# Three small jobs moved between engines, a later weight load and a new fixed order in an attention and FFT-MLP kernel

## The chip, the cores and the metric

The kernel runs on one core of one Trainium2 chip. The metric is the time of one execution in microseconds (us) on the device. Executions of one kernel mostly agree within a few tenths of a per cent to one per cent; now and then one is slower by over 1.5% (the slow state), and comparisons here use fast runs alone. TensorE multiplies matrices; VectorE, ScalarE and GpSimd (PE, DVE, ACT and POOL in the profile) do the rest; SyncE (SP) and GpSimd ask for transfers. "L926" is a line of the kernel. Where experiments have other line numbers, a longer order list has pushed the code down by six or seven lines.

## The reference, cut to what matters

```python
# attention, 4 batches, 8 heads, 768 tokens, 48 columns a head
for t in range(S):
    cur = einsum('bhd,bhe->bhde', u[None] * kt, vt)
    y[:, :, t] = einsum('bhd,bhde->bhe', rt, state + cur)
    state = wt[..., None] * state + einsum('bhd,bhe->bhde', kt, vt)
# x = y as (batch, 768, 384)
u  = x + real(fft(fft(x, axis=1), axis=2))          # mix over tokens and columns, residual
un = (u - mean(u)) / sqrt(var(u) + 1e-6)            # rows of 384
out = u + maximum(un @ w_ch1, 0) @ w_ch2            # w_ch1 is 384 x 1536, w_ch2 1536 x 384
```

## The kernel before

The recurrence is worked off in chunks of 128 tokens, six to a batch, c0 to c23. A chunk needs running sums of the logarithm of the decay w. The mix is done by matmuls with cosine and sine tables. Each row block of 128 tokens (n0 to n23) is then normed, transposed and multiplied with W1 and W2. Rows 15 to 17 and 21 to 23 are transposed by a DMA, the others by matmuls on TensorE. Four pieces concern us.

```python
# running sums of chunk n: one matmul, and a second one unless the chunk is in TCD
op("pe", "cum", ... matmul(ps(tce), MSK, L) ...)
if not tcd:
    op("pe", "cum", ... matmul(ps(tci), NLE, L) ...)           # L619
if tcd:
    op("dve", "tcd", ... tensor_tensor(out=e2, in0=ps(tce), in1=L, op=add) ...)   # L636
    op("act", "exp4", ...); op("act", "exp", ...); op("act", "expn", ...)
else:
    op("act", "exp2", ...)
# [...]
# row n: mix, residual, statistics, normed row, transpose, evacuation
op("pe", "mm", ...)                                            # 3 matmuls, L853
op("dve", "uf", ... add mix and residual ...)                  # L862
op("dve", "bns", ...); op("dve", "bna", ...)                   # L866, L868
op("act", "un", ... Identity(scale=-1, bias=agg mean) ...)     # L418
op("pe", "trn", ...); op("act", "ev384", ... unt <- bank ...)  # L889, L901
# [...]
ws, WN = [], ((6, "w"), (6, "w"))      # W1 and W2 are asked for after chunk 6's w load
```

Nothing is scheduled while the kernel runs. A list ORDER holds some 1,540 operations; every engine works off its own operations in the order of that list, and waits on semaphores where an input or a buffer isn't ready. BANKS says in which of eight PSUM banks each matmul result goes. A search made both lists.

Of the kernel before, what the change touches and what calls it, by code (L numbers as in the profile page):

```python
# [5 lines left out]
ALU = mybir.AluOpType  # L6
ACTF = mybir.ActivationFunctionType
# [5 lines left out]
    0, 3, 4, 74, 8, 9, 5, 7, 75, 17, 15, 13, 1, 39, 30, 76, 12, 18, 77, 24, 49, 11, 10, 47,  # L13
    31, 1511, 19, 59, 48, 40, 1512, 32, 1513, 20, 78, 1514, 41, 60, 22, 21, 109, 1515, 64, 25, 23, 1516, 61, 33,
    110, 34, 26, 35, 1517, 27, 28, 14, 63, 1518, 52, 29, 111, 55, 79, 36, 2, 38, 53, 6, 112, 56, 50, 51,
    37, 45, 81, 88, 141, 42, 43, 113, 46, 83, 92, 82, 142, 115, 54, 114, 84, 65, 85, 116, 117, 93, 143, 86,
    120, 80, 71, 118, 125, 87, 144, 124, 68, 89, 94, 119, 73, 126, 127, 173, 72, 96, 121, 44, 70, 102, 90, 95,
    145, 174, 103, 97, 57, 134, 129, 122, 175, 128, 98, 146, 58, 1519, 135, 123, 130, 99, 176, 69, 1520, 100, 152, 148,
    147, 131, 205, 177, 101, 1521, 66, 91, 178, 157, 179, 67, 206, 149, 1522, 133, 180, 153, 104, 150, 105, 132, 207, 151,
    156, 184, 159, 16, 158, 181, 106, 136, 208, 154, 182, 160, 166, 189, 185, 161, 137, 237, 167, 183, 209, 108, 191, 190,  # L20
    162, 211, 213, 238, 107, 210, 193, 155, 163, 138, 192, 239, 1523, 214, 139, 216, 266, 164, 215, 288, 194, 289, 290, 240,
    165, 212, 1524, 140, 195, 186, 217, 1525, 444, 241, 197, 291, 168, 188, 187, 169, 196, 445, 221, 198, 170, 267, 446, 222,
    1526, 220, 246, 1527, 171, 199, 242, 243, 447, 224, 244, 172, 218, 277, 200, 250, 251, 201, 226, 264, 245, 278, 1528, 202,
    252, 223, 247, 230, 203, 225, 292, 254, 231, 448, 253, 219, 268, 248, 256, 227, 1529, 255, 454, 228, 449, 293, 279, 451,
    229, 294, 257, 249, 458, 459, 295, 269, 232, 259, 204, 1530, 450, 455, 258, 452, 233, 453, 296, 297, 460, 280, 234, 456,
    270, 260, 281, 235, 1531, 261, 236, 461, 298, 299, 271, 463, 462, 262, 282, 272, 263, 300, 464, 273, 301, 283, 274, 302,
    265, 303, 304, 275, 284, 305, 285, 465, 286, 326, 276, 467, 317, 306, 308, 327, 457, 309, 466, 328, 318, 310, 329, 307,
    346, 468, 337, 311, 287, 319, 355, 1532, 330, 473, 1533, 312, 356, 474, 347, 331, 338, 313, 475, 332, 1534, 320, 339, 476,
    314, 321, 333, 471, 334, 357, 322, 1535, 340, 1536, 323, 315, 358, 316, 324, 469, 1537, 348, 325, 472, 1538, 1539, 378, 359,
    341, 372, 349, 366, 342, 368, 360, 470, 343, 350, 386, 369, 388, 351, 361, 382, 367, 389, 352, 362, 502, 62, 370, 379,  # L30
    376, 387, 384, 477, 377, 363, 353, 344, 374, 354, 345, 503, 380, 375, 479, 383, 419, 504, 373, 481, 483, 417, 385, 423,
    482, 505, 371, 484, 427, 381, 478, 531, 335, 395, 424, 489, 485, 336, 506, 415, 532, 480, 396, 486, 487, 488, 508, 533,
    418, 510, 428, 512, 491, 511, 490, 507, 421, 492, 534, 513, 390, 509, 493, 566, 517, 391, 535, 518, 514, 422, 497, 416,
    567, 519, 420, 515, 537, 499, 494, 568, 539, 520, 496, 541, 540, 397, 522, 495, 569, 392, 364, 542, 521, 536, 545, 500,
    601, 393, 547, 400, 570, 543, 538, 602, 498, 572, 516, 523, 544, 546, 574, 549, 398, 394, 401, 576, 551, 525, 548, 365,
    526, 603, 524, 550, 405, 577, 575, 528, 402, 604, 527, 605, 582, 578, 552, 501, 798, 607, 571, 411, 609, 579, 554, 799,
    584, 553, 413, 616, 586, 800, 403, 573, 558, 610, 406, 606, 409, 559, 801, 412, 407, 581, 608, 561, 414, 828, 615, 583,
    580, 425, 560, 585, 529, 829, 555, 564, 408, 562, 587, 410, 611, 830, 614, 617, 588, 434, 619, 530, 563, 618, 426, 399,
    429, 557, 809, 620, 612, 435, 802, 831, 556, 832, 565, 589, 648, 640, 621, 813, 613, 858, 649, 593, 623, 430, 810, 594,
    859, 641, 622, 590, 404, 596, 632, 431, 592, 591, 860, 833, 843, 834, 595, 624, 599, 439, 861, 597, 862, 625, 598, 440,  # L40
    811, 600, 888, 803, 835, 642, 633, 627, 804, 889, 650, 634, 651, 805, 643, 836, 436, 806, 890, 837, 626, 441, 807, 630,
    628, 808, 652, 653, 891, 635, 437, 629, 654, 636, 655, 637, 432, 631, 638, 644, 656, 838, 814, 815, 433, 645, 657, 680,
    646, 442, 658, 659, 662, 924, 816, 660, 844, 639, 671, 823, 818, 663, 845, 664, 824, 925, 681, 873, 682, 665, 846, 817,
    683, 647, 848, 672, 926, 700, 673, 666, 839, 819, 847, 709, 927, 684, 691, 849, 710, 701, 667, 661, 674, 820, 668, 960,
    692, 869, 685, 675, 693, 686, 669, 702, 825, 670, 443, 687, 676, 812, 822, 677, 850, 821, 688, 961, 840, 678, 711, 679,
    863, 703, 864, 826, 928, 962, 712, 899, 722, 892, 851, 734, 903, 963, 740, 865, 900, 689, 723, 438, 827, 738, 866, 868,
    852, 732, 870, 741, 1157, 867, 730, 841, 733, 720, 875, 694, 735, 1158, 726, 713, 964, 901, 935, 728, 731, 1159, 727, 704,
    742, 721, 1160, 695, 842, 724, 743, 871, 853, 877, 725, 1187, 874, 736, 969, 739, 714, 893, 854, 879, 856, 1188, 729, 883,
    936, 855, 876, 690, 894, 715, 744, 1189, 895, 878, 970, 705, 745, 884, 896, 737, 1190, 857, 880, 898, 872, 696, 749, 897,
    882, 1215, 697, 905, 750, 904, 1161, 885, 1216, 939, 929, 902, 930, 906, 937, 907, 908, 698, 971, 1217, 1168, 751, 909, 881,  # L50
    746, 706, 1218, 931, 972, 718, 910, 699, 747, 938, 754, 932, 934, 911, 748, 973, 707, 941, 716, 912, 933, 886, 1243, 708,
    913, 940, 755, 1169, 717, 752, 1244, 1191, 942, 916, 914, 944, 1198, 779, 1245, 887, 943, 1170, 780, 965, 1246, 759, 1199, 945,
    966, 765, 917, 760, 1277, 761, 967, 915, 919, 719, 949, 766, 1278, 767, 950, 968, 946, 918, 768, 763, 1279, 762, 947, 975,
    773, 1219, 951, 1280, 781, 1226, 948, 771, 782, 974, 753, 977, 1172, 923, 769, 1200, 764, 1162, 1227, 979, 1163, 1311, 976, 1164,
    952, 774, 777, 920, 1165, 978, 953, 921, 756, 770, 922, 1167, 980, 955, 757, 772, 999, 783, 778, 982, 758, 1174, 1202, 775,
    1312, 981, 1166, 1007, 1192, 776, 1000, 954, 1008, 991, 1009, 1193, 983, 1173, 957, 788, 1258, 984, 959, 992, 1194, 1182, 784, 986,
    1183, 1195, 1247, 1184, 789, 1230, 985, 1197, 1010, 1176, 956, 1175, 987, 1178, 785, 958, 989, 1177, 1001, 988, 1011, 993, 786, 994,
    1196, 995, 1012, 996, 990, 1002, 1013, 1179, 997, 1203, 1204, 1014, 1228, 1015, 1003, 1205, 1016, 1017, 1018, 1004, 1180, 790, 1005, 998,
    1181, 1019, 1039, 1288, 1021, 1206, 1030, 1281, 791, 1040, 1031, 1032, 1022, 1020, 1220, 1033, 1023, 792, 1041, 1006, 1059, 1024, 1068, 1313,
    793, 1171, 1034, 787, 1025, 1221, 794, 1035, 1042, 1036, 1207, 1026, 1043, 1027, 1069, 1037, 1060, 1209, 1070, 1038, 1061, 795, 1320, 1044,  # L60
    1062, 1045, 1028, 1071, 1050, 1051, 1029, 1289, 1222, 1046, 1052, 1048, 1210, 1047, 1208, 1248, 1249, 1223, 1185, 1225, 1095, 1053, 1224, 1232,
    796, 1079, 1096, 1101, 1231, 1254, 1234, 1097, 1250, 1186, 1087, 1253, 1054, 1081, 1080, 1260, 1233, 1088, 1063, 1083, 1251, 1102, 1055, 1211,
    1085, 1321, 1082, 1072, 1238, 1262, 1098, 1093, 1212, 1084, 1229, 1089, 1252, 1064, 1073, 1056, 1065, 1091, 1086, 797, 1259, 1255, 1099, 1239,
    1092, 1261, 1235, 1094, 1074, 1201, 1256, 1103, 1049, 1075, 1237, 1066, 1314, 1213, 1108, 1090, 1240, 1067, 1292, 1113, 1214, 1057, 1322, 1282,
    1100, 1283, 1076, 1236, 1263, 1109, 1284, 1290, 1104, 1058, 1287, 1265, 1285, 1315, 1294, 1110, 1286, 1264, 1114, 1257, 1293, 1296, 1316, 1105,
    1317, 1323, 1269, 1111, 1319, 1295, 1122, 1106, 1318, 1326, 1266, 1324, 1120, 1270, 1107, 1267, 1118, 1121, 1328, 1325, 1241, 1123, 1124, 1271,
# [221 lines left out]
def bass_rwkv6_finch__then__fnet_fourier_mix_kernel(  # L288
# [11 lines left out]
    DM = H * D  # L300
# [92 lines left out]
    def ps(t):  # L393
        return BANK[t.bank]
# [629 lines left out]
```

## Time and profile before

| | before |
|---|---|
| three runs, median (lowest to highest) | 196.43 us (195.55 to 197.74) |
| profiled span, clock of TensorE | 193.5 us, 1.000 of full |
| TensorE work and filler matmuls by the distance of their starts, idle | 157.5, 8.6, 24.7 us |
| first product with W1 | 43.9 us |
| W2 asked for, landed, first used | 36.5, 48.0, 52.7 us |

The prediction shows the lines. A group line reads: line, engine, operation, result from inputs, count, then total busy time in us and mean of one in ns, then the engine's idle time just before, and who ended it. To divide the whole span I use one more view, VectorE's start times: one residual add (L862) of each batch, the first one of batch 0 and that of row 0 of batches 1, 2 and 3. In the kernel before they come at 38.75, 83.98, 124.72 and 162.59 us, and the last matmul ends at 190.85. The recorded expectations call all of them first residual adds. That holds for batch 1; in batch 2 row 0's add is the second, and in batch 3 the third (the first ones come at 124.26 and 160.64 us). Where it matters, the text gives the first ones too.

### The profile page before, as it was taken

How to read it: one execution, taken by the hardware profiler on the slowest of the kernel's cores; microseconds unless marked ns; L12 is line 12 of the kernel's file. 1: busy time of each engine (PE TensorE's matmuls, PEld its weight loads, DVE VectorE, ACT ScalarE, POOL GpSimd, SP SyncE). 2: the span in 40 equal slices, each digit the busy share in tenths (PEclk: the TensorE clock that was granted, in tenths of full speed). 3: DMA queues.
4: the chain of work that ended last, by engine and by line, in shares of the span. 5: the costliest groups of instructions: out<-in, count | busy, mean ns of one | idle time of the engine just before them, and what ended most of it. 6: DMA issues, size and time to landing. Idle time of an engine off the chain costs nothing.

```text
span 193.5 us, 4590 instructions
## 1 busy us (share of the span) xinstructions
PE 180.0 (93%) x1730; PEld 114.7 (59%) x1730; DVE 152.1 (79%) x356; ACT 137.8 (71%) x333; POOL 118.3 (61%) x148
## 2 busy tenths in 40 slices
PE   4979899999999999998999998999979999979994
PEld 2446466755666566565767675666656566545663
DVE  8799689697258999999999999999989969800043
ACT  7899867656997794499999897488855344769400
POOL 1679789920689996899799988639375461000000
PEclk9999999999999999999999999999999999999999
DMA  5999899699989989889899991242735020140024
GB/s 118 225 217 188 170 218 172 116 179 201 208 176 237 207 176 244 160 193 233 186 211 227 199 226 32 54 125 54 160 68 122 3 81 2 38 149 0 0 81 163
DMA packets 113351, 28.14 MB, mean 145 GB/s; under 512 B 108209, under 2 KB 112946, under 8 KB 113330
## 3 DMA queue, kind: packets, MB, share of 16 engines
q1 hardware_dynamic: 111378, 25.50, 62.3%
q0 software_dynamic: 1952, 2.36, 7.4%
q8 instruction: 13, 0.21, 0.4%
q14 instruction: 8, 0.07, 0.1%
HBM read 23.59 MB, written 4.72 MB: 146 GB/s over the span
## 4 chain that ended last, share of the span: by engine, by line
PE 43%; DVE 34%; SPq 8%; DMA 6%; ACT 5%; issue 2%; DVEq 0%
PE bank L920 15%; PE bank L941 12%; SPq L440 7%; DVE ah L708 6%; DVE xf L404 5%; DVE x L862 4%; DVE osb L946 4%; DVE bst L866 3%; DMA unt<-un 3%; DMA in_w<-in_w_dram 3%; PE bank L821 3%; DVE x L773 2%; ACT ht L929 2%; DVE rh L663 2%; DVE xa L404 2%
## 5 line engine op out<-in xcount | busy, mean ns | idle before, releaser
L920 PE MATMUL bank<-unt,w 128*128 128x384 bf16 x288 | 52.5, 326 | 2.4 <-DMA unt<-un 2.4
L941 PE MATMUL bank<-w,ht 128*128 128x384 bf16 (+1 forms) x300 | 54.0, 320 | 0.2 <-DVE ah L708 0.2
L929 ACT ACTIVATE ht<-bank 128x384 bf16<-128x384 f32 x92 | 40.9, 505 | 9.8 <-PE bank L920 9.7
L920 PEld LDWEIGHTS bank<-unt,w 128*128 128x128 bf16 x288 | 26.4, 97 | 18.8 <-issue 3.2
L941 PEld LDWEIGHTS bank<-w,ht 128*128 128x128 bf16 x300 | 27.5, 98 | 15.3 <-DVE ah L708 0.4
L404 POOL TENSOR_TENSOR rk<-in_r,in_k 128x384 f32<-128x384 f32 x24 | 24.1, 1004 | 16.8 <-DMA in_r<-in_r_dram 15.8
L708 DVE TENSOR_TENSOR ah<-bank,msk 128x512 bf16<-128x512 f32 x48 | 31.2, 682 | 2.3 <-PE bank L703 2.2
L946 DVE SCALAR_TENSOR_TENSOR osb<-bank,rstd,x 128x384 f32<-128x384 f32 (+1 forms) x25 | 14.6, 595 | 21.7 <-PE bank L941 21.6
L404 POOL TENSOR_TENSOR rk<-rk,ub 128x384 f32<-128x384 f32 x24 | 24.2, 1013 | 0.6
L404 POOL TENSOR_TENSOR kh<-in_k,e 128x384 bf16<-128x384 f32 x18 | 18.3, 1019 | 5.8 <-ACT e L640 3.6
L404 POOL TENSOR_TENSOR vtd<-in_v,dc 128x384 f32<-128x384 f32 x24 | 19.8, 829 | 2.8 <-DVE dc L655 2.7
L663 DVE TENSOR_TENSOR rh<-bank,in_r 128x384 bf16<-128x384 f32 x24 | 13.2, 552 | 5.3 <-ACT bank L621 5.0
L418 ACT ACTIVATE un<-x,agg 128x384 bf16<-128x384 f32 x18 | 10.8, 619 | 9.3 <-DVE agg L868 9.1
L988 PE MATMUL bank<-wz 128*128 128x384 bf16 x53 | 13.8, 379 | 2.5 <-DVE wz L415 2.5
L655 DVE TENSOR_REDUCE dc<-rk 128x8 f32<-128x384 f32 x24 | 13.0, 545 | 1.9 <-POOL rk L404 1.8
L418 ACT ACTIVATE vb<-in_v 128x384 bf16<-128x384 f32 x24 | 12.7, 531 | 1.7 <-DMA in_v<-in_v_dram 1.2
L418 ACT ACTIVATE lb<-in_w 128x384 bf16<-128x384 f32 x24 | 12.6, 534 | 1.6 <-DMA in_w<-in_w_dram 1.3
L866 DVE BATCH_NORM_STATS2 bst<-x 128x6 f32<-128x384 f32 x24 | 12.7, 553 | 0.1
L821 PE MATMUL bank<-cs,xf 128*128 128x193 bf16 (+2 forms) x54 | 11.1, 257 | 1.4 <-DVE xf L404 1.2
L693 ACT ACTIVATE rtb<-bank 128x512 bf16<-128x512 bf16 x19 | 11.3, 605 | 1.4 <-PE bank L680 1.2
L862 DVE TENSOR_TENSOR x<-bank,x 128x384 f32<-128x384 f32 x24 | 12.3, 542 | 0.0
L695 ACT ACTIVATE ktb<-bank 128x512 bf16<-128x512 bf16 x19 | 11.2, 602 | 0.7 <-PE bank L684 0.7
(129 smaller groups left out, 362.3 us busy)
## 6 DMA issues: line engine op xcount, KB each, us to landing
in_w<-in_w_dram SPq DMA_DIRECT2D x24, 192.0 KB, 3.8
in_k<-in_k_dram SPq DMA_DIRECT2D x24, 192.0 KB, 3.8
in_r<-in_r_dram SPq DMA_DIRECT2D x24, 192.0 KB, 3.8
in_v<-in_v_dram SPq DMA_DIRECT2D x24, 192.0 KB, 3.9
out_dram<-osb SPq DMA_DIRECT2D x23, 192.0 KB, 2.3
w<-in_moe_w_ch_dram POOLq DMA_DIRECT2D x2, 1152.0 KB, 10.4
out_dram<-osb SPq DMA_DIRECT2D x2, 96.0 KB, 1.7
unt<-un SPq DMA_TRANSPOSE x6, 3.0
```

Of the source, the lines that this page charges most:

```text
L404: return shared(lambda e: e.tensor_tensor(out=o, in0=a, in1=b, op=f))
L418: return lambda e: e.activation(o, a, f, **kw)
L663: op("dve", "rh", lambda e: e.tensor_tensor(out=rh[:, :, 0:D], in0=ps(tce)[:, 0:DM].rearrange("t (h d) -> t h d", d=D), in1=rt[:, :, :], o ...
L708: masked[n] = op("dve", "ah", lambda e, x=x: e.tensor_tensor(out=ah[:, x:H:2, :], in0=ps(ta[x])[:, :].rearrange("p (h t) -> p h t", t=128) ...
L821: return e.matmul(ps(t)[:, k0:k1], xf[:, f, off:off + 128], tab[:, s, k0:k1], start=a, stop=z, skip_group_check=True)
L862: op("dve", "uf", lambda e, kb=kb, t=t: e.tensor_tensor(out=uf[:, kb, 0:DM], in0=ps(t)[:, 0:DM], in1=uf[:, kb, 0:DM], op=ALU.add), r=[t], ...
L866: op("dve", "bns", lambda e, kb=kb, bs=bs: e.bn_stats(bs[:, :], uf[:, kb, 0:DM]), r=[("X", b % 3, kb)], w=[("BST", n % 4)])
L920: ins = e.matmul(ps(t)[:, 0:384], W1[:, m, 128 * j:128 * j + 128], unt[:, m, :], start=(m == 0), stop=(m == NM - 1))
L929: op("act", "ev384", lambda e, j=j, t=t, ht=ht: e.activation(ht[:, j, :], ps(t)[:, 0:384], ACTF.Relu), r=[t], w=[("HT", q % 2, j)])
L941: ins = e.matmul(ps(t)[:, c0:c1], ht[:, j, 128 * x:128 * x + 128], W2[:, j, c0:c1], start=(j == 0), stop=(j == NJ - 1))
L946: op("dve", "osbh" if n_end else "osb", lambda e, kb=kb, t=t, o=o, c0=c0, c1=c1: e.scalar_tensor_tensor(out=o[:, c0:c1], in0=ps(t)[:, c0:c ...
L988: ins = e.matmul(ps(tw)[:, 0:384], WZ[:, 0:128], WZ[:, :])
```

## The change

It wants to take work off TensorE and ScalarE where batch 0's first normed rows stand between attention and the first product with W1. The wording of the change says that the decay sum is one of batch 0; in the code it is chunks 6 to 11, batch 1.

```diff
-    ws, WN = [], ((6, "w"), (6, "w"))
+    ws, WN, WG = [], ((6, "w"), (9, "w")), {7: "W1"}
-    KHD, DIAG, RKD, PRE, EVD = range(6), range(5), (), range(0), range(0)
+    KHD, DIAG, RKD, PRE, EVD, PRM = range(6), range(5), (), (), range(3), range(3)
-    TCD, SAD = range(12, 24), range(12, 24)
+    TCD, SAD = range(6, 24), range(12, 24)
@@ residual copy of the first three chunks
-            if n in PRE:
+            if n in PRE or n in PRM:
                 op("act", "xca", ... Copy, accum_out=XSUM ...)
                 op("dve", "tt1", ... XSUM *= 1/384 ...)
@@ mix: a 385th column brings the row mean of the mix
-                    w = DM + 1 if pre else DM
+                    w = DM + 1 if pre or n in PRM else DM
+            if n in PRM:
+                op("dve", "mean", ... MEAN = bank column 384 + XSUM ...)
@@ normed row
+                if n in PRM:
+                    op("act", "un", ... bias=MEAN ...)
-    NW2 = 5
+    NW2 = 6
@@ ORDER and BANKS: all new (1,540 operations before, 1,552 after); cut here
```

## The prediction

> **What bounds the kernel now.** I read the page first, then the chain that ended last, then the busy times by stretch, the waits, and the groups that the change touches. The page gives one core with a steady clock and a TensorE that looks almost full:
>
> ```profile
> PE 180.0 (93%) x1730; PEld 114.7 (59%) x1730; DVE 152.1 (79%) x356; ACT 137.8 (71%) x333; POOL 118.3 (61%) x148
> ...
> PE 43%; DVE 34%; SPq 8%; DMA 6%; ACT 5%; issue 2%; DVEq 0%
> ```
>
> Matmul busy time overlaps, so I took the distance between starts instead: back to back, a matmul of 384 columns starts every 0.162 us (the chain has 0.49 us for three, five times over). Adding such paces over all matmuls gives about 157.5 us of needed work and 8.6 us of filler matmuls (53 on a tile of zeros, 0.162 us each). The last matmul ends at 190.8, so TensorE idles about 24.7 us: 10.8 before 40 us, 1.3 from 40 to 60, 4.8 from 60 to 90, 7.8 after. The chain's second name is VectorE, and the stretches say why:
>
> ```profile
> 44.00:60.00 16.00, 16.00 (x133) 10.08 (x133) 8.31 (x20) 13.88 (x36) 8.93 (x10) 1.00 1.06 199
> 60.00:88.00 28.00, 26.65 (x302) 17.28 (x300) 27.24 (x58) 20.67 (x48) 25.48 (x31) 1.00 0.96 202
> 88.00:113.00 25.00, 24.68 (x275) 16.47 (x270) 24.61 (x53) 23.97 (x64) 23.45 (x26) 1.00 1.01 210
> 113.00:131.00 18.00, 17.05 (x179) 11.29 (x177) 17.66 (x38) 12.60 (x30) 11.87 (x16) 1.00 0.41 99
> 131.00:144.00 13.00, 12.22 (x113) 7.61 (x111) 12.66 (x31) 9.82 (x26) 9.28 (x11) 1.00 0.44 95
> ```
>
> The columns after the stretch and its length are PE, PEld, DVE, ACT and POOL busy time. From 60 to 144 VectorE works 82.2 of 84 us: there TensorE and VectorE bound the kernel together. Only from 44 to 60 is VectorE half empty (7.7 us idle). So two things count: what the change takes from TensorE, and whether VectorE's added work fits into that hole.
>
> The stage that the change aims at is the first normed rows of batch 0:
>
> ```profile
> 38.83 0.93 DVE x L862 x2
> 39.76 0.93 DVE bst L866 x2
> 40.80 1.12 ACT un L418 x2
> ...
> 42.90 0.34 PE bank L889 x3
> 43.91 3.57 PE bank L920 x21
> ```
>
> Residual, statistics, normed row, transpose, then the first product with W1 at 43.9. Behind it the second weight crowds the loads of batch 1:
>
> ```profile
> POOL rk L404 <- DMA in_r<-in_r_dram: 15.8, 5, 9.2
> ...
> DMA to landing us min/median/max: 11.6/11.6/11.6
> ```
>
> The second line is W2, asked for at 36.5 and landed at 48.0. A load of k asked for at 37.2 landed only at 47.4, and GpSimd stood still for 9.2 us until r of chunk 7 came at 48.8. That is what leaves VectorE's hole.
>
> **What the Trainium skill says.**
> - "Perfetto Trace Analysis", section Identifying the Most-Contended Engine, says matmul busy share is a poor measure of TensorE's headroom while occupancy is fair for the others. The trace agrees: 180.0 us busy against 166 us by pace.
> - "ScalarE: Activation LUTs", section What ACT_TABLE_LOAD costs, gives 186 ns + 0.833 ns per element for an ACTIVATE with immediates and about 93 ns more per pointer operand: 506 and 599 ns at 384 columns. The trace has 492 and 619 ns.
> - "VectorE: DVE Perf Modes", section Why PSUM operands drop a tier, holds fp32 from PSUM to one element a cycle, so a copy from PSUM is no cheaper on VectorE. The trace agrees: VectorE's relu from PSUM takes 553 ns, ScalarE's copy 492.
> - "DMA: Bandwidth & Descriptors", section Issuing engines are not separate DMA queues, says transfers of all issuers interleave on the same 16 engines. The k load's 10.2 us beside W2, against a median of 3.8, agrees.
>
> **The change part by part.** The durations:
>
> ```profile
> L619 PE MATMUL bank<-lb,nle 128*128 128x384 bf16 x12 | 3.9, 329 | 0.8 <-ACT lb L418 0.8
> ...
> L636 DVE TENSOR_TENSOR e<-bank,lb 128x384 f32<-128x384 f32 x12 | 6.6, 551 | 0.2
> ...
> L640 ACT ACTIVATE e<-bank 128x8 f32<-128x8 f32 (+1 forms) x10 | 1.8, 181 | 3.9 <-DVE e L636 3.9
> ...
> L901 ACT ACTIVATE unt<-bank 128x384 bf16<-128x384 f32 x18 | 8.2, 492 | 0.2
> ...
> L872 DVE TENSOR_SCALAR mean<-agg 128x1 f32<-128x1 f32 x6 | 0.8, 147 | 0.0
> ...
> L925 DVE TENSOR_SCALAR ht<-bank 128x384 bf16<-128x384 f32 x4 | 2.2, 553 | 1.5 <-PE bank L920 1.5
> ```
>
> 1. Decay sum of chunks 6 to 11 (in the code that is batch 1). Six second cumulative matmuls go: 6 x 0.162 = 0.97 us off TensorE, and a PSUM bank each. Six VectorE adds come: 6 x 0.551 = 3.3 us. ScalarE keeps its two exponentials and gets five small ones, 5 x 0.18 = 0.9 us more: it is not relieved here.
> 2. Evacuation of the first three transposed rows: 3 x 0.492 = 1.5 us leave ScalarE, 3 x 0.55 = 1.65 us come to VectorE.
> 3. Row means: three copies get a sum output (cost unknown here; I take 0.1 us each), VectorE gets three scalings and three adds of one column, 6 x 0.15 = 0.9 us; nine matmuls get a 385th column, under 0.01 us. The normed row no longer waits for its two statistics. In the chain 0.93 us of statistics and the last aggregate go, 0.15 to 0.3 us for the means come. The transposed row then queues on VectorE. Going step by step from the same 38.8 (add, add, mean at 39.9; rows on ScalarE to 41.3; statistics 0.55; copies to 42.9), W1 starts near 43.0 instead of 43.9: 0.9 us.
> 4. W2 waits for the w load of chunk 9 instead of 6. Loads without it land some 0.87 us apart here, so chunk 9's w comes near 46. In the new order GpSimd must also do k-hat of chunk 7 and two products first, each about 1 us, so I put the request at 46 to 50 and, with 10 to 11.6 us, the landing at 57 to 61.
> 5. One more filler matmul, 0.16 us, in idle time.
> 6. The order. I counted the new list off against the operations in program order. The first product with W2 moves from position 171 to 199 in TensorE's order: 17.2 us of paced work now lie between the first W1 product and it, not 8.7. So W2 is wanted near 61, and attention of batch 1 fills in before. The last stage keeps its 24.4 us of TensorE work after the last transpose by matmul.
>
> Sum for VectorE: 3.3 + 1.65 + 0.9 = 5.85 us more, about 1 us of it before 38 us and the rest where 7.7 us are free. So the saturated stretch can start at most some 3 us ahead; with 1.5 to 2 us of new idle left it is about 1 us ahead. Adding VectorE's new list from the first row mean to the last fold of batch 1 gives 41.3 us, 38.8 to 80.1 if never idle, against 80.8 in the trace: again at most about 1 us. ScalarE's list from the first normed row to the last relu of that batch half is 32.3 us against 31.6, so it is nearly full from 40 to 72 and lets nothing run further ahead. TensorE: 0.97 less work, part of which VectorE's pace takes back. I put the net gain at 1.6 us: 196.4 - 1.6 = 194.8.
>
> **The rivals.**
> - *The hole was the cost, and everything shifts.* If batch 1 flows without gaps, the 0.9 of the chain, the 0.97 of TensorE and half of the 4.8 us of TensorE idle from 60 to 90 come off: 4 us, 192.2. For it: the 9.2 us wait is real. Against: 5.85 us of new VectorE work goes into a hole of 7.7.
> - *W2 comes late, or starves the loads of chunk 10.* These are next in the queue when it starts, and the new order puts their transposes just before W2's first use. A stall of 1 to 3 us in batch 1 would make 195.5 to 198. For it: what the k load shows. Against: the order was made with this in mind.
> - *VectorE saturates sooner and pays it all back.* The gain at 43 us is lost by 80: 196 to 196.5. The near tie of 80.1 and 80.8 speaks for it.
> - *Early or late reordering alone moves it.* Before 40 us there are 10.8 us of idle; a better first stage would give another 1 us either way.
>
> **Range and chances.** These are 192.2 at the good end and about 198 at the bad; repeated runs of the kernel before spread 195.5 to 197.7. I take 192.6 to 197.2. Over 2% faster means under 192.5: only the first rival, 0.11. Over 2% slower means above 200.4: a stall beyond anything seen in this stage, 0.03. Within 2%: 0.86.
>
> **What would show it.** Right: L619 has 6 instead of 12 and the L636 group 18; the first W1 product starts near 43; W2 asked for between 46 and 50; GpSimd's long wait for r gone; VectorE over 80% busy from 44 to 60 and still full from 60 to 144. Wrong: TensorE waiting on W2 or on chunk 10's rows near 60 (slower), or VectorE no longer full after 60 and TensorE's idle there halved (faster than I say), or a first W1 product that does not move.

## The result and the profile after

The changed kernel takes 189.38 us (189.23 to 190.37, four runs), the kernel before 197.09 beside it (195.55 to 199.55, four runs, of which 199.55 counts as slow and isn't in the ratio). The ratio is 0.9644, with a 95% interval from 0.9578 to 0.9709: faster, and outside the predicted range. A ratio is the mean time of one kernel's fast runs over that of the other's fast runs of the same rounds, so it isn't quite the ratio of the medians quoted. Later repeats gave 0.975 and 0.970.

The page of the changed kernel, busy times and the chain that ended last:

```profile
PE 179.4 (95%) x1725; PEld 115.1 (61%) x1725; DVE 156.6 (83%) x371; ACT 138.1 (73%) x339; POOL 118.0 (63%) x148
...
PE 71%; DVE 13%; ACT 11%; DMA 2%; issue 2%; DVEq 0%; ACTq 0%
```

Before, the chain was 43% TensorE and 34% VectorE. Now it is 71% TensorE: the end is followed back through matmuls that wait for nothing but each other. VectorE has 4.5 us more to do and is a smaller part of the chain.

The same stretches as before (stretch and length, then PE, PEld, DVE, ACT and POOL busy time, clock, DMA share and GB/s):

```profile
44.00:60.00 16.00, 15.72 (x173) 9.74 (x170) 15.12 (x38) 15.98 (x43) 12.22 (x14) 1.00 1.16 195
60.00:88.00 28.00, 27.17 (x278) 17.65 (x277) 25.05 (x56) 19.23 (x46) 24.57 (x30) 1.00 0.96 197
...
131.00:144.00 13.00, 13.00 (x135) 8.38 (x134) 12.88 (x32) 8.16 (x22) 11.38 (x14) 1.00 0.38 74
```

VectorE's hole from 44 to 60 us is filled: 15.12 us busy, where it was 8.31. From 60 to 88 it has 2.95 us free, where it had 0.76. From 131 to 144 TensorE no longer pauses.

The first normed rows, in the chain of waits (start, length, engine, what):

```profile
39.84 0.49 PE bank L853 x3
40.33 0.33 PE bank L895 x6
...
42.17 1.15 PE bank L926 x6
```

The chain no longer passes through statistics and normed row on VectorE and ScalarE. The first product with W1 starts at 42.17, 3.85 us after the first residual add (38.32); before it was 5.16 us (38.75 to 43.91). Then the waits (what waited for what, in total, times, longest) and W2's landing:

```profile
POOL rk L404 <- DMA in_r<-in_r_dram: 7.2, 4, 4.1
...
DMA to landing us min/median/max: 12.8/12.8/12.8
```

GpSimd's long wait of 9.2 us for r is gone: r of chunk 7 lands at 42.12, not 48.80. W2 was asked for at 49.09 and landed at 61.91; TensorE first uses it at 62.44. The groups show the moved work:

```profile
L636 DVE TENSOR_TENSOR e<-bank,lb 128x384 f32<-128x384 f32 x18 | 9.8, 546 | 0.2
...
L619 PE MATMUL bank<-lb,nle 128*128 128x384 bf16 x6 | 2.1, 343 | 0.2 <-ACT lb L418 0.2
```

Where did the time go? The stretches between these residual adds of the batches tell. First the kernel before, then the changed one:

```profile
38.75:83.98 45.23, 43.76 (x433) 27.93 (x432) 36.81 (x81) 33.69 (x82) 31.35 (x38) 1.00 1.03 198
83.98:124.72 40.74, 39.30 (x424) 25.96 (x423) 39.91 (x84) 35.86 (x90) 36.41 (x44) 1.00 0.83 174
124.72:162.59 37.87, 35.99 (x343) 22.83 (x342) 34.16 (x76) 21.68 (x54) 21.71 (x27) 1.00 0.34 82
```

```profile
38.32:82.14 43.82, 43.19 (x433) 27.61 (x431) 39.90 (x91) 32.56 (x82) 31.55 (x37) 1.00 1.02 193
82.14:121.74 39.60, 38.64 (x418) 25.58 (x416) 38.69 (x82) 36.23 (x89) 35.34 (x43) 1.00 0.91 192
121.74:157.18 35.44, 35.44 (x342) 22.51 (x341) 33.12 (x75) 20.97 (x54) 23.07 (x29) 1.00 0.38 90
```

Up to the add of batch 1 the changed kernel gains 1.84 us (83.98 against 82.14). Then it gains 1.14 us and 2.43 us in two stretches in which no part of the change but the order differs. In the last of these TensorE is busy through all of its 35.44 us, with the same number of matmuls within one. The tail loses 0.5 us in this trace; a wait of 1.1 us for a DMA-transposed row is in it (1.2 in the kernel before), which two later traces don't have. The spans differ by 4.9 us: 1.84 + 1.14 + 2.43 - 0.5. The last two terms depend on the mark: at the first add of batch 3 (160.64 against 155.77 us) the last stretch has gained 1.89, and the tail behind it is as long as before (30.20 and 30.17 us). The order's part is thus 3.0 us at the first adds and 3.6 at row 0's.

So over 60% of the gain lies where the prediction gave nothing. That can be the order's work (theory O), or the lead of the early half that grows by itself (theory H), or the sum of the parts, showing late.

### The profile page after: what moved, and what is told of

The parts are those of the page before. It is cut to its first block, busy times and chain, and to the rows that moved or that the text cites. A ratio compares the mean times of both kernels' runs of the same rounds, so it can differ in the third digit from the quotient of the medians.

```text
span 188.6 us, 4611 instructions
## 1 busy us (share of the span) xinstructions
PE 179.4 (95%) x1725; PEld 115.1 (61%) x1725; DVE 156.6 (83%) x371; ACT 138.1 (73%) x339; POOL 118.0 (63%) x148
## 4 chain that ended last, share of the span: by engine, by line
PE 71%; DVE 13%; ACT 11%; DMA 2%; issue 2%; DVEq 0%; ACTq 0%
PE bank L947 21%; PE bank L926 19%; PE bank L853 5%; PE bank L821 5%; DVE ah L708 4%; PE bank L703 3%; PE bank L994 2%; DMA unt<-un 2%; PE bank L684 2%; PE bank L749 2%; DVE xf L404 2%; PE bank L680 2%; PE bank L753 2%; PE bank L895 1%; PE bank L720 1%
## 5 line engine op out<-in xcount | busy, mean ns | idle before, releaser
L926 PE MATMUL bank<-unt,w 128*128 128x384 bf16 x288 | 53.2, 326 | 1.4 <-DMA unt<-un 1.1
L935 ACT ACTIVATE ht<-bank 128x384 bf16<-128x384 f32 x92 | 40.8, 502 | 11.6 <-PE bank L926 11.4
L926 PEld LDWEIGHTS bank<-unt,w 128*128 128x128 bf16 x288 | 25.9, 97 | 18.2 <-issue 2.1
L404 POOL TENSOR_TENSOR xd<-x 128x385 f32<-128x385 f32 x9 | 10.2, 1133 | 6.3 <-DVE x L773 6.2
L655 DVE TENSOR_REDUCE dc<-rk 128x8 f32<-128x384 f32 x24 | 12.8, 542 | 1.5 <-POOL rk L404 1.4
L693 ACT ACTIVATE rtb<-bank 128x512 bf16<-128x512 bf16 x19 | 11.6, 608 | 3.2 <-PE bank L680 2.9
L642 ACT ACTIVATE e<-e 128x384 f32<-128x384 f32 x18 | 9.4, 529 | 5.2 <-DVE e L636 5.2
L418 ACT ACTIVATE un<-x,agg 128x384 bf16<-128x384 f32 x15 | 9.2, 623 | 4.9 <-DVE agg L871 4.8
```

Source lines behind the costliest of these rows:

```text
L404: return shared(lambda e: e.tensor_tensor(out=o, in0=a, in1=b, op=f))
L418: return lambda e: e.activation(o, a, f, **kw)
L655: op("dve", "dc", lambda e: e.tensor_reduce(out=dc[:, :], in_=rku[:, :, :], axis=mybir.AxisListType.X, op=ALU.add), r=[("RK", i2)], w=[("D ...
L926: ins = e.matmul(ps(t)[:, 0:384], W1[:, m, 128 * j:128 * j + 128], unt[:, m, :], start=(m == 0), stop=(m == NM - 1))
L935: op("act", "ev384", lambda e, j=j, t=t, ht=ht: e.activation(ht[:, j, :], ps(t)[:, 0:384], ACTF.Relu), r=[t], w=[("HT", q % 2, j)])
```

## The experiments

Eighteen runs were made, all correct: fourteen new kernels, two of them twice, and the changed kernel twice more. A part's stretch is a sharper measure than its time: the new order gave the same stretches within 0.05 us where nothing else was changed (one of 40.50 in ctrl_after apart), while the start of a run wandered by 1 us. The old order nearly did so too, but for its last stretch (36.82 to 38.72 us); "One late wait by itself" says why. Each row is one trace. This table has every fast profile. The columns are the first residual add, the three stretches between the adds of row 0 (batch 0: the first add), the stretch from there to the end of the last matmul, and the ratio to the kernel before.

| kernel | first add | to batch 1 | to batch 2 | to batch 3 | to the end | ratio, 95% interval |
|---|---|---|---|---|---|---|
| before | 38.75 | 45.23 | 40.74 | 37.87 | 28.26 | 1 |
| changed | 38.32 | 43.82 | 39.60 | 35.44 | 28.76 | 0.964, 0.958 to 0.971 |
| ctrl_after | 39.31 | 43.80 | 40.50 | 35.45 | 27.47 | 0.975, 0.972 to 0.978 |
| after_again | 38.52 | 43.82 | 39.59 | 35.44 | 27.47 | 0.970, 0.965 to 0.975 |
| early_new | 38.52 | 43.84 | 41.23 | 37.63 | 26.86 | 0.993, 0.984 to 1.002 |
| mid_new | 38.16 | 43.81 | 41.09 | 37.42 | 26.86 | 0.981, 0.977 to 0.984 |
| late_again | 38.60 | 45.63 | 39.95 | 35.44 | 28.67 | 0.990, 0.985 to 0.995 |
| only_b2 | 39.24 | 45.67 | 41.47 | 37.23 | 28.12 | 1.005, 1.001 to 1.009 |
| only_b3 | 38.88 | 45.28 | 40.75 | 36.11 | 29.01 | 0.995, 0.989 to 1.000 |
| no_evd | 38.14 | 43.66 | 39.58 | 35.44 | 27.48 | 0.969, 0.965 to 0.973 |
| no_prm | 38.51 | 45.71 | 39.59 | 35.44 | 27.48 | 0.980, 0.971 to 0.989 |
| no_tcd | 39.66 | 47.11 | 39.59 | 35.44 | 28.46 | 1.001, 0.993 to 1.008 |
| w2_early | 40.32 | 49.29 | 39.60 | 35.44 | 27.47 | 1.004, 0.995 to 1.013 |
| prm_old | 39.27 | 46.30 | 40.74 | 36.82 | 28.00 | 1.004, 0.998 to 1.010 |
| parts_old | 40.89 | 54.22 | 40.75 | 37.53 | 26.86 | 1.042, 1.036 to 1.048 |
| w2_late | 38.91 | 59.04 | 40.74 | 38.72 | 28.25 | 1.071, 1.065 to 1.076 |
| un15_first | 39.05 | 45.30 | 40.74 | 38.01 | 28.24 | 1.000, 0.997 to 1.003 |
| un15_early | 37.92 | 45.25 | 40.74 | 38.73 | 28.15 | 1.011, 1.007 to 1.016 |

### The order split in time

**early_new** takes the changed kernel's program and order up to the first residual add of batch 1, and the old order behind it.

```diff
-ORDER: the changed kernel's
+ORDER: the changed kernel's up to the first residual add of batch 1, then that of before
+BANKS: 14 results in another bank, where the old one was taken at the seam
```

> The changed kernel's program and order up to the first residual add of batch 1, then the order of the kernel before for batches 2 and 3. Two theories. O (order of the later batches): the first half alone is worth the 1.8 us by which that add starts earlier in the changed trace, the rest comes from the new order of batches 2 and 3, so this run is 1.5 to 2.5 us faster than before (ratio 0.987 to 0.992). H (hole): work moved forward into VectorE's hole from 44 to 60 is the whole cause and the lead grows by itself, so this run keeps 6 us or more (ratio under 0.970).

Its median was 194.53 us (192.53 to 195.85), before 195.06. The early stretch is the new one, 43.84 us, but then 41.23 and 37.63 follow, as long as in the kernel before or nearly so. The lead doesn't grow by itself: theory H, which asked for a ratio under 0.970, falls, and so does the sum of the parts that shows late, since all the parts are in this kernel. The interval of this ratio (0.984 to 1.002) reaches 1, so the early half's own gain in time isn't clear of noise.

**late_new** and **late_again** are the other half: old program, old order up to the same add, new order behind it.

```diff
-ORDER: that of before
+ORDER: that of before up to the first residual add of batch 1, then the changed kernel's
+BANKS: 5 results in another bank
```

> The kernel before up to the first residual add of batch 1, then the new order for batches 2 and 3. O: it gains what the first half doesn't, 4 to 6 us (ratio 0.970 to 0.980). H: the new late order needs the early lead and is worth under 1 us here (ratio over 0.995). If both halves gain about half each, the parts simply add up.

It took 193.35 us (192.89 to 198.59), ratio 0.990, interval 0.983 to 0.997.

> A repeat of the kernel with the old program and order up to the first residual add of batch 1 and the new order behind it, because its profile fell in the slow state. Theory O: in a fast profile that add comes near 84.0 as in the kernel before, the stretch to batch 2 takes 39.6 to 40.0 us and the one to batch 3 35.4, and the time is 2.0 to 3.4 us under that of before, ratio 0.983 to 0.990. Rival (the stretches of the slow profile were short because the slow start had given the other engines a lead): 40.7 and 37.9 us again, ratio above 0.993.

The repeat took 193.45 us, before 195.86, ratio 0.990. Its two later stretches:

```profile
84.23:124.18 39.95, 38.64 (x418) 25.53 (x416) 38.87 (x82) 36.03 (x89) 34.77 (x43) 1.00 0.86 179
124.18:159.62 35.44, 35.44 (x342) 22.51 (x340) 33.12 (x75) 20.96 (x54) 23.07 (x29) 1.00 0.39 90
```

The second line repeats the changed kernel's line almost digit by digit: TensorE 35.44 of 35.44 us, VectorE 33.12. None of the change's parts is in this kernel. The late gain is that of the order, with the banks that go with it: 2.6 us by the spans (193.5 and 190.9) and 2.0 us by the ratio.

**mid_new** carries the new order on to batch 2.

```diff
-ORDER: the changed kernel's
+ORDER: the changed kernel's up to the first residual add of batch 2, then that of before
+BANKS: 8 results in another bank
```

> The changed kernel's program and order up to the first residual add of batch 2, then the order of before for the rest. O (order of the later batches): batch 1 to batch 2 takes 39.6 us as in the changed kernel, batch 2 to batch 3 takes 37.7 us as in the kernel before instead of 35.4, TensorE waits over 1 us again for the third transposed row of batch 2, and the time is 1.5 to 2.5 us over the changed kernel. H (hole): the lead carries on by itself, batch 2 to batch 3 takes about 35.4 us and the time is within 0.7 us of the changed kernel.

Its median was 191.65 us, before 195.34. The last stretch is back at 37.42 us, 2.0 longer than with the new order (35.44). The stretch before it seems to miss what was expected, 41.09 and not 39.6, but that is the mark: row 0's add is the first operation behind the seam, where the two orders are joined. The first add of batch 2, still in the new order, comes after 39.12 us, as in the changed kernel (39.14). Two things did miss: the kernel is only 1.1 us slower than ctrl_after by the medians, not 1.5 to 2.5, and TensorE's wait for the third transposed row is 0.3 us, not over 1. Instead TensorE stands still for 0.86 and 0.33 us right behind the seam, so part of the loss may be the seam's.

**only_b3** and **only_b2** put one of the late stretches of the new order in the old list.

```diff
 ORDER: that of before
+only_b3: from the first residual add of batch 2 on, the changed kernel's (4 banks changed)
+only_b2: between the first residual adds of batches 1 and 2, the changed kernel's (13 banks changed)
```

> The program of the kernel before, in its own order up to the first residual add of batch 2 and in the changed kernel's order from there on. Theory O (the new order of the later batches gains by itself, mostly between the first residual adds of batches 2 and 3): that stretch takes 35.4 us instead of 37.9 and the time falls by about 2.4 us, ratio near 0.988. Theory of my prediction (the order of late batches is worth nothing, the gain is made before 90 us): the stretch keeps 37 to 38 us and the ratio is within 0.996 to 1.004.

> The program of the kernel before, with the changed kernel's order only between the first residual adds of batches 1 and 2. Theory O: that stretch takes 39.6 us instead of 40.7, the time falls by about 1 us, ratio near 0.995. Rival (only the last batch's order matters, or the stretch's gain is given back behind the seam, where the old order resumes): ratio 0.998 to 1.003.

With only_b3 the stretch fell from 37.87 to 36.11, most of what was expected, and the time to 194.24 us from 195.46. The interval just reaches 1. With only_b2 the kernel was slower by 0.9 us (196.34). The 41.47 us of its stretch are again the seam's mark: the first add of batch 2 comes after 39.49 us, 0.78 earlier than in the kernel before (40.27) and just as in late_again. But then 37.27 us follow to the first add of batch 3, where the kernel before takes 36.39. So the rival for only_b2 was right: the gain appears and is given back behind the seam, with the same two pauses of TensorE (0.87 and 0.33 us) as in mid_new. This piece of the new order is worth nothing alone. Before the new last stretch it is worth something: 40.75 + 36.11 = 76.86 us in only_b3, 39.95 + 35.44 = 75.39 in late_again. The pieces aren't independent, and a seam costs something too; the runs don't separate these two.

### One part undone in the new order

These use the changed program and order; the operation that comes back stands where its replacement stood. The exception is no_prm, where the statistics of the three rows also move up, to right behind each residual add. **ctrl_after** is the changed kernel unaltered.

> The changed kernel itself once more, as the yardstick on this chip for the other runs of this group. Both theories: 0.960 to 0.972 of before. Its first residual adds of batches 1, 2 and 3 should again start near 82.1, 121.7 and 157.2 us in the trace; if the starts of batch 3 or the end scatter by more than 1 us, the last stage isn't as steady as one trace makes it look.

190.53 us against 195.34: ratio 0.975, so the first measurement of the gain was on the high side.

```diff
 no_evd:   -EVD = range(3)      +EVD = ()              # evacuation back on ScalarE
 no_prm:   -PRM = range(3)      +PRM = ()              # means from the statistics
 no_tcd:   -TCD = range(6, 24)  +TCD = range(12, 24)   # second matmul again (44 banks changed)
 w2_early: -WN = (6,w),(9,w)    +WN = (6,w),(6,w)      # W2 asked for with W1
```

> The changed kernel with the first three transposed rows copied out by ScalarE again, at the same places of the order. If ScalarE is the full engine from 40 to 60, as the changed trace says (15.98 of 16 us busy), the 1.5 us come back in whole or in part: 0.7 to 1.5 us slower than the changed kernel. If only the chain counts, a copy of 0.49 us on ScalarE against 0.55 on VectorE makes no difference (under 0.3 us).

It took 189.18 us, not slower. The stretch is 0.16 us shorter than with the evacuation on VectorE. Was this the better kernel? It was measured again beside the changed one.

> A repeat of the changed kernel with the evacuation of the first three transposed rows back on ScalarE, beside the changed kernel itself, to see whether it beats it. Theory that the evacuation's engine is worth 0.2 us in the stage and the rest of the first difference was jitter of the start: the two agree within 0.5 us. Rival (it is the better kernel): faster than the changed kernel by 1 us or more, ratio to before at least 0.005 lower.

> The changed kernel again, as the measure for the run beside it and as a third estimate of the whole gain: 189.2 to 190.6 us, ratio to before 0.965 to 0.975, with the stretches between the first residual adds of 43.8, 39.6 to 40.5 and 35.4 us.

This time it took 190.27 us and the changed kernel 189.40 (before 196.16). The sign turned, so no difference between the two is shown, and there is no version here that beats the changed kernel. One execution of no_evd_again took 452.5 us; it is left out, and the last section tells what it looked like.

> The changed kernel with the first three row means taken from the batch statistics again (statistics put right behind each residual add on VectorE, no sum outputs, no mean adds). If the short cut of the normed-row chain is worth the 0.9 us that the prediction gave it, this is 0.7 to 1.2 us slower than the changed kernel (ratio to before about 0.969); if the chain is hidden by other work, no difference (0.964).

It took 191.50 us. The first stretch is 45.71 us, 1.9 longer than 43.8, and more than the 0.7 to 1.2 that I expected. So in the new order the row means are worth up to 1.9 us; the earlier statistics on VectorE are in this number.

> The changed kernel with chunks 6 to 11 taking the inclusive decay sum by a second matmul again: 0.97 us more TensorE work, 3.3 us less on VectorE, small exponentials gone from ScalarE (0.9 us), a PSUM bank more held. If TensorE's work is what counts: 0.5 to 1.2 us slower than the changed kernel. If VectorE's fullness counts: up to 1 us faster. If PSUM banks are short in this order: 1 to 3 us slower, with TensorE waiting on evacuations from 44 to 80 us.

It took 195.01 us, as slow as the kernel before and 4.5 us slower than ctrl_after. The stretch is 47.11 us, 3.3 longer; of what I expected, only the case of short PSUM banks (1 to 3 us) comes near. From 44 to 60 us VectorE was busy for 11.76 us and TensorE for 14.45. Its list had to change 44 banks, because six more results need one, so some of these 3.3 us may be the price of a list not made for it.

> The changed kernel with W2 asked for as early as before (after the w load of chunk 6), its place in GpSimd's queue moved up, all else unchanged. H: chunk 7's k, r, v land near 48 again, GpSimd and TensorE stall, and 4 us or more of the gain are lost (ratio over 0.985). O: the stall costs the early lead only, 1 to 3 us (ratio 0.970 to 0.980). If the late request did nothing: ratio 0.964 as the changed kernel.

It took 196.44 us; the stretch is 49.29, 5.5 longer. The waits between 30 and 60 us:

```profile
ACT lb L425 <- DMA in_w<-in_w_dram: 6.0, 1, 6.0
...
PE bank L621 <- ACT lb L425: 3.8, 1, 3.8
```

ScalarE waited 6.0 us for w of chunk 7, which had been asked for at 39.16 and landed at 48.54 behind W1 and W2, and TensorE waited for ScalarE. In the new order attention of batch 1 stands where the old one had products with W2, so its loads mustn't be late. The loads aren't the whole 5.5 us. After TensorE had stood still, from about 45 to 49 us, its granted clock was low, 0.79, 0.50 and 0.85 in the three stretches of 2 us from 48 on, where the changed kernel has 1.00 from 44 to 60:

```profile
50.00:52.00 2.00, 2.00 (x8) 0.92 (x7) 1.97 (x6) 1.20 (x3) 0.21 (x1) 0.50 1.09 206
```

With the shares of full clock that are missing while it works, that is 1.7 us by estimate.

### The parts in the old order

**w2_late** changes nothing of the kernel before but W2's request.

```diff
-ws, WN = [], ((6, "w"), (6, "w"))
+ws, WN = [], ((6, "w"), (9, "w"))      # and its place in GpSimd's list: after chunk 8's product of r and k
```

> The kernel before with W2 alone asked for late, after chunk 9's w load, everything else in the old order. Theory that the late request pays only with the new order: r of chunk 7 lands near 42 instead of 48.8 and GpSimd's long wait goes, but the first W2 product stands at position 171 of TensorE's list and waits for W2 until 58 to 62, so TensorE stands still for 3 to 8 us there and the kernel is slower by 1 to 6 us, ratio 1.005 to 1.03. Rival (the late request by itself brings the early gain): ratio 0.99 to 0.995.

It took 209.6 us, 14 more than before and far more than I had expected. GpSimd came to the request only at 55.08 us, W2 landed at 64.95, and the old order wanted it at 52.7:

```profile
PE bank L947 <- DMA w<-in_moe_w_ch_dram: 12.1, 1, 12.1
...
66.00:68.00 2.00, 2.00 (x8) 0.96 (x7) 0.00 (x0) 0.00 (x0) 0.00 (x0) 0.50 0.04 8
```

The second line is of the stretches: behind the wait the granted clock is 0.50 until 68 us and 0.87 on average from there to 70, which costs 1.7 us more by estimate. The two make up the 13.8 us by which the first stretch grew. An earlier place in GpSimd's list wasn't tried, so this run prices a late W2 in the old order, not the new condition by itself.

**prm_old** adds row means and VectorE's evacuation to the old order; **parts_old** adds the decay sums too. Each new operation stands where the one stood that it replaces.

```diff
 prm_old:   +EVD, PRM = range(3), range(3)
 parts_old: +EVD, PRM, TCD = range(3), range(3), range(6, 24)
 both: W2 asked for early; the sixth filler matmul kept; the last table operation moved ahead of
 the first mix matmul, which now reads it
```

> The row means and the evacuation on VectorE alone, each new operation where the one stood that it replaces; the order, W2's request and the decay sums are the old ones. Theory that the shorter chain needs the new order: the first W1 product comes 0.9 to 1.3 us after where the residual add leads it, near 42.7, but the first residual adds of batches 1, 2 and 3 stay within 0.4 us of the old 84.0, 124.7 and 162.6, ratio 0.997 to 1.003. Theory of my prediction (the 0.9 us of the chain is worth most of itself by itself): these adds come 0.7 to 1.2 us earlier, ratio near 0.995.

The first product with W1 started at 45.31 us, later than in the kernel before, and not at the 42.7 that I expected. The chain says why:

```profile
42.52 0.46 DVE unt L909
...
44.70 0.47 DVE unt L909
...
45.31 1.78 PE bank L933 x10
```

The third evacuation waits on VectorE until 44.70, since the old list has statistics and residual adds of other rows ahead of it. The evacuation moved into a queue, and the old order left it at the back. The time was 196.28 us against 195.86: nothing gained.

> All parts but W2's late request in the old order: row means, evacuation, and the decay sums of chunks 6 to 11 on VectorE; three of the sums and their neighbours had to move by 10 to 30 positions, because their buffers come free late. Theory that the parts pay only with the order made for them: ratio 0.998 to 1.01, and the stretch between the first residual adds of batches 0 and 1 stays at 45 us or grows, since the hole of VectorE from 44 to 60 us is still a wait for r of chunk 7. Theory of my prediction (1.6 us from these parts, the order worth nothing): ratio 0.99 to 0.994.

203.64 us, 8 more than before. VectorE is busy for only 9.20 us from 44 to 60, so the hole isn't filled. TensorE now waits for k-hat rows (3.4 us in all), GpSimd for exponentials and ScalarE for the decay sums on VectorE:

```profile
ACT e L647 <- DVE e L643: 13.5, 8, 5.5
POOL kh L411 <- ACT e L649: 13.4, 8, 5.2
```

The sum's buffer is freed late by the chunk three before it, so three sums had to move back by 10 to 30 positions, and attention of batch 1 came late. Placed like this in the old order, the parts that my prediction counted don't gain 1.6 us. They lose.

### One late wait by itself

What in the new order shortens the last stretch? In the kernel before, the chain there stops at a DMA-transposed row (start, length, what):

```profile
138.31 0.51 ACT un L418
...
139.43 2.38 SPq L882
...
141.85 2.38 DMA unt<-un
...
144.37 0.65 PE bank L920 x3
```

ScalarE makes chunk 15's normed row last of three, SyncE's queue takes them one behind the other, and TensorE stands still for 1.15 us until the third has landed. In the changed kernel the same row is first: the three transposes are asked for at 133.96, 135.26 and 136.56 and have landed by 140.15, 4.1 us earlier (3.0 of it is the lead that this kernel has by the first add of batch 2), and TensorE has no wait there. **un15_first** and **un15_early** move this row alone.

```diff
 ORDER: that of before
+un15_first: row 15 normed and sent ahead of rows 16 and 17
+un15_early: row 15 normed as soon as its mean is there, and sent at once
```

> The kernel before with one thing reordered in batch 2: of the three rows that are transposed by DMA, chunk 15's normed row is made and sent first, as in the changed kernel, not last. If TensorE's wait of 1.3 us for the third transposed row at 144 us is what the new order of batch 2 to 3 removes, the stretch between the first residual adds of batches 2 and 3 falls from 37.9 to about 36.5 and the time by 1.0 to 1.3 us, ratio near 0.994. If the wait is only where slack shows (VectorE's work after it sets the pace), the wait at 144 us goes, others take its place, the stretch stays at 37.5 to 38 and the ratio is 0.998 to 1.002.

It took 195.47 us, ratio 1.000. But the row came only at 136.8, for the place on ScalarE that I had given it waits for another row's mean, and 0.84 us of the wait was left. This doesn't decide.

> The kernel before with chunk 15's normed row made as soon as its mean is there (near 135 us, not at 138.2) and its DMA transpose right behind it; the first try had moved it only to 136.8 and left 1.0 us of TensorE's wait at 144 us. If that wait is part of what the new order removes between batches 2 and 3, it falls under 0.5 us, and the stretch between the first residual adds of batches 2 and 3 falls from 37.9 to about 37.0, ratio near 0.995. If VectorE sets the pace there, the wait goes and the stretch stays within 0.2 us of 37.9, ratio 0.998 to 1.002.

The row came at 134.2 us, and the wait at 144 was gone. The median was 197.72 us against 196.16, ratio 1.011: slower. Neither theory foresaw that. The profiled run was the fastest, 195.23 us, where the other fast ones took 197.39 to 197.99, so its trace shows only part of the loss: the stretch is 38.73 us, 0.86 longer. The chain shows where the wait went:

```profile
138.50 1.89 issue
140.39 0.40 PE bank L709 x8
```

L709 is a product of attention whose row is transposed by a DMA of the same queue. With row 15 ahead of it, that row landed at 140.30 and no longer at 138.66. Counted from the first add of batch 2 it came 2.4 us later (16.85 and 14.40 us). This suggests that the queue has room for the three rows early only if attention's rows are placed to match: the changed kernel's list asks for none of them between 132.72 and 139.34 us. So the wait belongs to what the new order removes, but moving one operation doesn't remove it.

What the wait is worth can be read from the traces with the old order in this stretch, because it differs from trace to trace with the landing of the transposes. TensorE's wait on a DMA-transposed row is 0 in prm_old, 0.64 in early_new, 0.83 in parts_old, 0.84 in un15_first, 1.15 in the kernel before, 1.89 in un15_early and 1.98 in w2_late. Take it from the stretch, and 36.7 to 37.2 us are left in all seven. So the wait lengthens the stretch by about its own length, 1.15 of the 2.43 us here. The same DMA landings also move the last stretch of a single trace by up to 1.9 us. The other 1.3 us are the new order's too: in prm_old, with no such wait, the stretch is 36.82 us and not 35.44.

## Why the prediction was wrong

**The bound** was read rightly: TensorE and VectorE share it from 60 us on, and the hole before is W2's doing.

**The parts' counts and places** came true: L619 6 times, L636 18 times, W2 asked for at 49.1 (46 to 50 said), GpSimd's wait gone, VectorE 95% busy from 44 to 60. W2 landed at 61.9, just past the 57 to 61, and took 12.8 us, not 10 to 11.6. The product with W1 came 1.74 us earlier, not 0.9: 0.43 of it is an earlier residual add, and the chain is 1.3 us shorter.

**The gain by batch 1's first add** was 1.84 us in the first trace, 1.64 in after_again and 0.87 in ctrl_after, where the start alone differs; about the 1.6 that was predicted for the whole. That is luck, for the route to it was wrong. I summed parts, but parts_old shows that the same parts in the old order cost 8 us, and w2_late that a late W2 alone costs 14. In the new order, taking back row means, sums or the late request costs 1.9, 3.3 or 5.5 us (1.7 of the last by the clock) in a stretch that gains 1.4 in all. These numbers can't be added up: each measures what its lack does to a list made for it. The evacuation, counted at 1.5 us of ScalarE, is worth nothing that the runs can show.

**The step that failed is the sixth, the order.** I counted one product's place in it and wrote "The last stage keeps its 24.4 us", which is so for the tail (30.20 and 30.17 us from the first add of batch 3 to the last matmul); the rivals then gave reordering "another 1 us either way", before 40 us only. For the two stretches from batch 1 to batch 3 I put down nothing, because VectorE looked full there and kept its work, though my own count had 7.8 us of TensorE's idle time after 90 us. The traces show 3.57 us gained in them (1.14 + 2.43; 3.03 at the first adds), and late_again, with none of the parts, shows 0.79 + 2.43 (2.68). VectorE's fullness was the wrong test. It was busy for 34.16 of 37.87 us in the last of these stretches and so had 3.7 us of waits; now it has 2.3, and TensorE's pauses are gone. By the distances of matmul starts TensorE idled for some 4 us in this stretch and now for less than 2, an estimate. The chain that went back and forth between the two engines (43% and 34%) held waits that a better order took out, though the work stayed the same.

**The rival** "The hole was the cost, and everything shifts" was priced at 192.2, nearer to the result than my own figure, and for another reason than the runs show: the hole was filled, but only 1.84 us had come of it by the first add of batch 1. Of its sign, "VectorE no longer full after 60 and TensorE's idle there halved", the first half came true; TensorE's idle from 60 to 90 fell from 4.8 to about 3.2 us by estimate. The rival of starved loads was half right: v of chunk 10 and w of chunk 11 took 11.9 and 11.1 us beside W2, but from 50 to 70 us no engine waits for a load.

**Open.** The halves bring 1.4 us (early_new, not clear of noise) and 2.0 us (late_again) by their ratios, 3.4 in sum, the whole 4.9 to 7.0. Order and banks changed together and weren't taken apart. Seams with changed banks lose some of it in each half, but how much is a seam and how much the fit of early to late can't be told from these runs. Nor do they tell which rearrangements make up the 2.4 us of the last stretch, beyond the 1.15 us of the row transposes above.

## What to carry to other kernels

When a change comes with a new fixed order, don't price the order at nothing: find the stretches in which two engines take turns in the chain, and count the waits that are left in them as what it can win at most; here the order won 3.0 to 3.6 us of the 4.9 us in the first traces. Try a part in the old order before crediting it: a part moved to another engine joins a queue, and here the row means were worth up to 1.9 us in the list made for them and nothing in the old one, where all three parts together lost 8 us. If a wait is to be removed by moving one operation, look first at what it will then stand in front of. And where lists are joined, put a mark on the near side of the seam.

## What the Trainium skill lacked or had wrong

- "TensorE: Matmul & The Clock Gate", section Wait — 56ns, not 53.3ns?, puts the spacing of matmuls at N / 2.4 GHz + 2.5 ns when warm, 162.5 ns at 384 columns, and at N / 1.2 GHz when cold, 320 ns. The changed kernel agrees with the first: its products with W2 start 162 ns apart in the median. Neither fits what one execution of no_evd_again showed. It took 452.5 us, the same products started 432 ns apart, and the mean granted clock was recorded as 1.0. Its group line (busy us, mean ns; in the other traces the mean is 319 or 320, in w2_late 324):

```profile
L954 PE MATMUL bank<-w,ht 128*128 128x384 bf16 (+1 forms) x300 | 137.5, 669 | 0.0
```

  The other five runs of that kernel took 189.34 to 191.58 us. Only TensorE was slow: in the same trace the products of VectorE with the mask took 682 ns and ScalarE's relus 490 ns in the median, as in no_evd (681 and 494). The cause stays open; the page does warn, in section Seeing it yourself, that records of the clock can be unreliable.
- "DMA: Bandwidth & Descriptors" (section Latency and other measured facts for the figure below) lacks how much a large transfer holds back small ones asked for beside it: a load of 192 KB takes 3.7 to 3.9 us in the median, but one of k took 10.2 us beside W2's 1152 KB in the kernel before, and w of chunk 7 took 9.4 us in w2_early. It gives transposes by DMA an effective 261 GB/s, measured on one kernel with a non-contiguous middle dimension; at that rate a row of 128 x 384 in bf16 (96 KB) would take 0.38 us by estimate, a transfer's fixed cost left out. It has no time for one small transpose or for several in a row. Here one takes 2.4 us from issue to landing when alone, and three behind each other had landed after 6.1 us.
- No page has the cost of the sum output of an ACTIVATE. The trace shows a second instruction behind each, of 242 ns on average, where I had put 100 ns:

```profile
L766 ACT ACTIVATION_READ_ACCUMULATOR x<-bank 128x1 f32 x3 | 0.7, 242 | 0.0
```
